# The operands of a pass made over two units, and two products changed about in the last unit

## The chip, the cores and the metric

The kernel runs on one core of a Trainium2 chip. Its engines work side by side, each on its own queue of instructions in a fixed order: TensorE (PE in the profile) multiplies, VectorE (DVE) and ScalarE (ACT) work element by element, GpSimd (POOL) and SyncE (SP) mostly issue DMAs here. An instruction waits until what it reads is there and until the buffer that it writes is free, and everything behind it on the same engine waits with it. The metric is the device time of one execution in microseconds (us); the times given are medians of several executions. One more execution was recorded by the profiler, and all rows in this document come from such recordings.

## The reference

Three networks stand behind one another. Cut to what matters, the computation is:

```python
x = attention(q, k, v)               # 4 x 8 heads x 576 x 64, local and strided masks
x = routed_experts(x, ...)           # 2304 tokens, 512 wide, 8 experts, one for each token
h = np.maximum(x @ w_in, 0.0)        # second network: 512 -> 2048
return (h * h @ w_out).astype(np.float32)   # 2048 -> 512
```

All the change lies in the last two lines: x has 2304 rows of 512, w_in is 512 x 2048, w_out is 2048 x 512.

## The kernel before

**Passes and units.** The second network runs in three passes, g = 0, 1, 2, of six tiles of 128 tokens each, in two halves of three tiles (384 tokens). A pass has eight units, c = 0 to 7; a unit computes 256 of the 2048 hidden columns and adds their part of the output. The trace names things of a unit by its number: m_7S is a product of unit 7, gl_7_10 an operand made from one of its results.

**Seven products.** A unit multiplies a 2 x 2 block matrix of weights (two blocks of 128 columns by two of 256 inputs) with a 2 x 2 block matrix of tokens, by a scheme of seven products of sums instead of eight: in this order A11·B11, S2·T2, A12·B21, S3·T3, S1·T1, A22·T4, S4·B22. In the trace m_7A is a product with a plain block A, m_7S one with a sum S. Each is six matmuls of 128 x 384 (function `mm3`, lines 1119 to 1121: every factor is a high part and a low part, and three of the four pairs are multiplied). The products lie in PSUM in two buffers, so that the sixth product may start only when what reads the fourth is done, and the seventh when what reads the fifth is done. VectorE joins the products with sums u (`add`, four tiles u[0] to u[3]): u[2] reads the fourth product, u[3] is the second reader of the fifth. In the trace all four are called u.

**Four results.** Four results, named by (i, hf) as 10, 01, 00, 11, go through `squared` (line 1432): VectorE adds a u into rl, ScalarE takes the relu and the square, gh is its high part (ScalarE), gl its low part (VectorE). Result 10 hangs on the third product, 01 on the fifth, 00 on the sixth, 11 on the seventh.

**The output.** `down` multiplies gh and gl with two rows of w_out (hwo, lwo: high and low part) into six PSUM tiles o_0 to o_5, one for each token tile, 36 matmuls of 128 x 512 in a unit; they accumulate over the eight units. These steps are spread through the next unit's products, as its `q()` calls come to them. With the last of them a tile is scaled into an SBUF buffer ob (even tiles on ScalarE, odd ones on VectorE), and POOL writes it to its rows of the output with an indirect DMA. There are five ob buffers, so a pass's sixth ob (ob_5) waits until the DMA of the first one has landed:

```python
ob = late.tile([P, D], F32, name=f"ob{g}_{t}", tag="ob", bufs=5)
```

**Operands of a pass.** The token sums of a pass are made by `split2(g, part)` from the transposed activations y2T: part 0 makes B11 and T2, part 1 B21 and T3, part 2 T1 and T4, part 3 B22. High parts (xh, xbh) are made by ScalarE, sums (xs) and low parts (xl, xbl) by VectorE; parts 0 to 2 take 2 xs or 4 xs of 384, one xl of 768 and two xl of 384, part 3 one xbl of 768. No DMA is in them. They are called in unit 7 of the pass before.

**Weights.** The weights of a unit come by DMA from a scratch in DRAM (SyncE's queue) and are split into high and low parts, hwa, hwb, hwo by ScalarE and lwa (128 x 1024), lwb (768), lwo (1024) by VectorE (line 1099).

**What sets the order.** The code is traced into a list, and a scheduler orders each engine's queue by its own estimates; `issue_after` and `keep_in_program_order` bind it in places. So a step that is called later may pull others with it.

Of the kernel before, what the change touches and what calls it, by code (L numbers as in the profile page):

```python
# [20 lines left out]
P = 128  # L21
# [6 lines left out]
F2 = 2048  # L28
# [5 lines left out]
UC = 256  # L34
# [21 lines left out]
MG = [(3, 3), (3, 3), (3, 3)]  # L56
# [75 lines left out]
def moe_kernel(ctx, tc, q, k, v, wg, wog, w1, w2, w_in64, w_out64, consts, out, dbg=None):  # L132
# [105 lines left out]
    lead = {}  # L238
# [630 lines left out]
    for b in range(B):  # L869
        t = tiles[b]  # L870
        tn = transposes(b + 1, tiles[b + 1]) if b + 1 < B else iter(())
        for n, ku in enumerate(ORDER[b].split()):
            kind, u = ku[0], int(ku[1:])
# [229 lines left out]
    def get(u):  # L1103
        assert u in ready
        return ready[u]

    def ahead(u, n, m=None, far=None):
        i = units.index(u)
        while nxt[0] < min(i + (far or n), len(units)):
            if nxt[0] >= i + n and units[nxt[0]][0] not in ("w1", "w2"):  # L1110
                break
            prep_unit(units[nxt[0]])
            nxt[0] += 1
        while cut[0] < min(i + (m or n), nxt[0]):
            split_unit(units[cut[0]])
            cut[0] += 1

    def mm3(ps, ah, al, bh, bl_, first, last, kept=lambda ins: ins):
        kept(nc.tensor.matmul(ps, ah, bh, start=first, stop=False))  # L1119
        kept(nc.tensor.matmul(ps, ah, bl_, start=False, stop=False))  # L1120
        lead["sum"] = kept(nc.tensor.matmul(ps, al, bh, start=False, stop=last))  # L1121
# [265 lines left out]
    for k in range(E):  # L1387
        for f in range(NF1):
# [22 lines left out]
            if (k, f) in CONV:  # L1411
                n = CONV.index((k, f))
# [5 lines left out]
            if f == (7 if k == 0 else 4) and k + 1 < E:  # L1418
                if k:
                    win_split(k + 1)  # L1420
                else:
                    a = pend.pop(0)
# [59 lines left out]
    def quarters(g, c, hs):  # L1482

        n = MG[g][0]
        if (g, c) == (len(MG) - 1, F2 // UC - 1):

            by = dict(hs)
            steps = [(i, 0, t) for i in (1, 0) for t in range(n)] + [(i, 1, t) for t in range(n, 2 * n) for i in (0, 1)]
            for i, hf, t in steps:
                yield lambda i=i, hf=hf, t=t: down(  # L1490
                    g, c * (UC // P) + i, [t], hf * n, by[i, hf], False, i == hf, tc.keep_in_program_order
                )
            return
        for (i, hf), h in hs:
            ts = range(hf * n, hf * n + n)
            first = c == 0 and (i, hf) in ((1, 0), (0, 1))
            last = c == F2 // UC - 1 and (i, hf) in ((0, 0), (1, 1))
            yield lambda i=i, ts=ts, h=h, a=first, b=last: down(g, c * (UC // P) + i, ts, ts[0], h, a, b)

    def m_unit(g, c, todo):  # L1500


        HC = MG[g][0] * P
        def preps(n):
            gate = lead.get("gate")
            with ExitStack() as st:
                for ins in gate or ():
                    st.enter_context(tc.issue_after(ins.ins))
                ahead(("wa", g, c), n)

        preps(3 if g + c == 0 else 5)
        wa, wb = get(("wa", g, c)), get(("wb", g, c))
        X = x2[g]
        q = lambda: next(todo, lambda: None)()
        end = c == F2 // UC - 1 and g + 1 < len(MG)

        def nxt_(part):
            if end:
                with tc.issue_after(lead["sq"][0].ins), tc.issue_after(lead["sq"][1].ins):
                    split2(g + 1, part)  # L1520

        def prod(w, x):
            j = BLK[w] - 1
            (wh, wl), j = (wa, j) if j < 4 else (wb, j - 4)
            xh, xl = X[x]
            ps = psm.tile([P, 512], F32, name=f"m{g}_{c}{w}", tag="h", bufs=2)
            for a in range(2):
                s_ = slice(a * P, (a + 1) * P)
                mm3(ps[:, :HC], wh[:, j, s_], wl[:, j, s_], xh[:, a], xl[:, a], a == 0, a == 1)
            return ps  # L1530

        u = [raws.tile([P, 3 * P], F32, name=f"u{i}{g}_{c}", tag="win", bufs=4)[:, :HC] for i in range(4)]
        add = lambda o, ps, x: nc.vector.tensor_tensor(o, ps[:, :HC], x, op=ALU.add)
        hs = []
        put = lambda i, hf, *a: hs.append(((i, hf), squared(f"{g}_{c}_{i}{hf}", *a)))
        p = prod("A11", "B11")
        nc.scalar.activation(u[0], p[:, :HC], AF.Copy)
        p = prod("S2", "T2")
        add(u[1], p, u[0])
        nxt_(0)  # L1540
        q()
        p = prod("A12", "B21")
        put(1, 0, p, HC, u[0])
        p = prod("S3", "T3")
        add(u[2], p, u[1])
        nxt_(1)
        q()
        p = prod("S1", "T1")
        put(0, 1, p, HC, u[2])
        if g == 0:  # L1550
            lead["gate"] = lead["sq"]
        else:
            lead.pop("gate", None)
        if g + c == 0:
            preps(5)
        add(u[3], p, u[1])
        p = prod("A22", "T4")
        put(0, 0, p, HC, u[2])
        nxt_(2)
        q()  # L1560
        p = prod("S4", "B22")
        put(1, 1, p, HC, u[3])
        nxt_(3)
        q()
        return quarters(g, c, hs)

    todo = iter([lambda a=a, d=d: e_l2(*a, range(d, d + 2)) for a in pend for d in (0, 2)])
    for g in range(len(MG)):
# [181 lines left out]
```

## Time and profile before

| what | value |
|---|---|
| median of 3 executions (lowest, highest) | 774.67 us (774.64, 775.0) |
| the profiled execution's own time | 773.4 us |
| its span, first to last instruction | 771.6 us |
| granted TensorE clock, mean | 0.998 of full speed |
| busy: PE, DVE, ACT, POOL | 98%, 72%, 60%, 22% of the span |

The span is what the rows count; 1.8 us of the execution lie outside it. PE is busy nearly all the time at nearly full clock, so the few places where it waits in the second network are what an order of work can change. Busy shares of the others are means over the whole run; near a change of pass they are much higher. The output's last DMA is issued by POOL at the end of the third pass.

### The profile page before, as it was taken

Reading aid. Unit: us, or ns where it says so; the run is one execution under the profiler, and the core shown is the slowest. Engines: PE = TensorE matmul, PEld = TensorE weight load, DVE = VectorE, ACT = ScalarE, POOL = GpSimd, SP = SyncE. Lnnn points to the kernel's source line nnn. Section 1 sums busy time; section 2 is a strip of 40 time slices with the busy share of each in tenths; the row PEclk is TensorE's granted clock in tenths of the full one; section 3 lists DMA queues with packets and bytes.
Section 4 is the critical chain, followed back from the end, with each engine's and each line's share of the span. In section 5 each row is a group of like instructions: output and inputs, shape, how many; then the busy total and the mean of one; then the engine's idle time right before and its main releaser. Section 6 shows DMA issues by size and latency. Waiting matters only on the chain.

```text
span 771.6 us, 14519 instructions
## 1 busy us (share of the span) xinstructions
PE 755.5 (98%) x5436; PEld 678.8 (88%) x5436; DVE 558.3 (72%) x1069; ACT 462.0 (60%) x935; POOL 171.5 (22%) x168
## 2 busy tenths in 40 slices
PE   8999999999999999999999999899999999999995
PEld 5777777999999999999988989788899888989894
DVE  4777787965676888898799888995455697555442
ACT  2764656425555555666687667785556676565443
POOL 6100002046528534320122222141000003000003
PEclk9999999999999999999999999999999999999999
DMA  9899715594988998965454544434222234222002
GB/s 207 170 199 228 143 58 152 185 299 146 202 265 192 329 282 277 305 205 183 157 205 151 177 148 171 157 136 157 91 76 96 86 118 159 78 93 103 1 0 84
DMA packets 104114, 124.86 MB, mean 162 GB/s; under 512 B 39428, under 2 KB 76856, under 8 KB 104040
## 3 DMA queue, kind: packets, MB, share of 16 engines
q1 hardware_dynamic: 95736, 100.42, 45.4%
q0 software_dynamic: 7568, 22.70, 8.9%
q8 instruction: 44, 0.72, 0.4%
q10 hardware_dynamic: 736, 0.76, 0.4%
q14 instruction: 30, 0.25, 0.1%
HBM read 101.82 MB, written 22.04 MB: 161 GB/s over the span
## 4 chain that ended last, share of the span: by engine, by line
PE 58%; issue 31%; DVE 6%; POOL 2%; DMA 1%; ACT 1%; SPq 0%; POOLq 0%; DVEq 0%; ACTq 0%
PE y L1119 5%; PE y L1121 5%; PE y L1120 5%; PE h L1119 5%; PE h L1121 5%; PE h L1120 5%; PE o L1120 2%; PE o L1119 2%; PE o L1121 2%; PE rw L566 2%; POOL out_dram L1471 2%; PE idle L232 1%; PE wt L1203 1%; PE lr L748 1%; PE sc2l L387 1%
## 5 line engine op out<-in xcount | busy, mean ns | idle before, releaser
L1119 PE MATMUL o<-hwo,gh 128*128 128x512 f32 x288 | 113.6, 396 | 0.4 <-ACT gh L1441 0.4
L1120 PE MATMUL o<-lwo,gh 128*128 128x512 f32 x288 | 113.5, 395 | 0.0
L1438 ACT ACTIVATE rl<-rl 128x384 f32<-128x384 f32 x96 | 49.6, 516 | 86.8 <-DVE rl L1436 86.8
L1099 DVE TENSOR_TENSOR lw<-rw,hw 128x1024 fp32r<-128x1024 f32 x62 | 83.0, 1341 | 16.3 <-ACT hw L1095 16.1
L1121 PE MATMUL o<-hwo,gl 128*128 128x512 f32 x288 | 84.2, 395 | 0.7 <-DVE gl L1443 0.7
L1119 PE MATMUL h<-xh,hw 128*128 128x416 f32 (+7 forms) x256 | 80.4, 315 | 0.2 <-DVE hl L1313 0.2
L1443 DVE TENSOR_TENSOR gl<-rl,gh 128x384 fp32r<-128x384 f32 x96 | 55.9, 585 | 32.6 <-ACT rl L1442 32.2
L1121 PE MATMUL h<-xh,lw 128*128 128x416 f32 (+7 forms) x256 | 79.3, 310 | 0.0
L1120 PE MATMUL h<-xl,hw 128*128 128x416 f32 (+7 forms) x256 | 79.3, 310 | 0.0
L1471 POOL DMA_INDIRECT out_dram<-ob,idx x18 | 23.1, 1284 | 252.3 <-ACT ob L1470 247.2
L1120 PE MATMUL y<-hl,hw 128*128 128x416 f32 (+7 forms) x256 | 78.6, 310 | 0.0
L1121 PE MATMUL y<-hh,lw 128*128 128x416 f32 (+7 forms) x256 | 78.1, 310 | 0.0
L1311 ACT ACTIVATE hh<-h 128x416 fp32r<-128x416 f32 (+7 forms) x64 | 28.2, 440 | 81.5 <-PE h L1121 81.5
L1119 PE MATMUL y<-hh,hw 128*128 128x416 f32 (+7 forms) x256 | 74.2, 311 | 0.0
L1095 ACT ACTIVATE hw<-rw 128x1024 fp32r<-128x1024 f32 x62 | 65.1, 1054 | 4.1 <-PE h L1120 3.8
L1119 PEld LDWEIGHTS o<-hwo,gh 128*128 128x128 f32 x288 | 54.0, 188 | 10.8 <-ACT gh L1441 1.2
L1120 PEld LDWEIGHTS o<-lwo,gh 128*128 128x128 f32 x288 | 54.1, 188 | 10.0 <-DVE lwo L1099 0.5
L1121 PEld LDWEIGHTS o<-hwo,gl 128*128 128x128 f32 x288 | 53.4, 188 | 8.7 <-DVE gl L1443 1.1
L1442 ACT ACTIVATE rl<-rl 128x384 f32<-128x384 f32 x96 | 50.1, 522 | 2.2
L1313 DVE SCALAR_TENSOR_TENSOR hl<-h,hh 128x416 fp32r<-128x416 f32 (+7 forms) x64 | 31.3, 489 | 27.5 <-ACT hh L1311 27.3
L1441 ACT ACTIVATE gh<-rl 128x384 fp32r<-128x384 f32 x96 | 50.0, 521 | 1.9
L1119 PEld LDWEIGHTS h<-xh,hw 128*128 128x128 f32 x256 | 48.2, 188 | 0.7 <-DVE hl L1313 0.5
(628 smaller groups left out, 1922.1 us busy)
## 6 DMA issues: line engine op xcount, KB each, us to landing
rw<-in_moe_w_dram SPq DMA_DIRECT2D x62, 512.0 KB, 5.7
rwa<-ws_d SPq DMA_DIRECT2D x24, 512.0 KB, 3.4
rwb<-ws_d SPq DMA_DIRECT2D x24, 384.0 KB, 3.2
e6wi<-in_moe_w_in_dram SPq DMA_DIRECT2D x32, 256.0 KB, 5.9
rwo<-wout_d SPq DMA_DIRECT2D x16, 512.0 KB, 3.6
x_d<-xr SPq DMA_DIRECT2D x18, 256.0 KB, 4.7
ws_d<-eo POOLq DMA_DIRECT2D x16, 256.0 KB, 5.2
s0wo<-in_moe_w_out_dram SPq DMA_DIRECT2D x8, 512.0 KB
```

Of the source, the lines that this page charges most:

```text
L1095: ia = nc.scalar.activation(hi, raw, AF.Copy)
L1099: iv = eng.tensor_tensor(lo, raw, hi.bitcast(F32), op=ALU.subtract)
L1119: kept(nc.tensor.matmul(ps, ah, bh, start=first, stop=False))
L1120: kept(nc.tensor.matmul(ps, ah, bl_, start=False, stop=False))
L1121: lead["sum"] = kept(nc.tensor.matmul(ps, al, bh, start=False, stop=last))
L1311: lead["relu"] = nc.scalar.activation(hh[:, :C], ps[:, :C], AF.Relu)
L1313: lead["step"] = nc.vector.scalar_tensor_tensor(out=hl[:, :C], in0=ps[:, :C], scalar=0.0, in1=hh[:, :C].bitcast(F32), op0=ALU.max, op1=ALU ...
L1438: nc.scalar.activation(rl[:, :HC], src, AF.Relu)
L1441: nc.scalar.activation(hh[:, :HC], rl[:, :HC], AF.Square)
L1442: ia = nc.scalar.activation(rl[:, :HC], rl[:, :HC], AF.Square)
L1443: iv = nc.vector.tensor_tensor(hl[:, :HC], rl[:, :HC], hh[:, :HC].bitcast(F32), op=ALU.subtract)
L1471: ins = nc.gpsimd.indirect_dma_start(out=out[:, :], out_offset=bass.IndirectOffsetOnAxis(ap=idx[:, gt_, 0:1], axis=0), in_=ob, in_offset=None,
```

## The change

Two things change. First, at the two changes of pass, only parts 0 and 1 of the next pass's operands are still called in unit 7 (at the first and the third of four places); parts 2 and 3 are called in the first unit of the new pass, at its first two places. Second, in the very last unit of the kernel the fifth and sixth products change places (A22·T4 comes before S1·T1), four steps of `down` are taken ahead of the seventh product, and the twelve last steps of `down` stand in another order.

```diff
--- before.py
+++ after.py
@@ -1484,11 +1484,12 @@
         n = MG[g][0]
         if (g, c) == (len(MG) - 1, F2 // UC - 1):
 
-            by = dict(hs)
-            steps = [(i, 0, t) for i in (1, 0) for t in range(n)] + [(i, 1, t) for t in range(n, 2 * n) for i in (0, 1)]
+            a, b, c_ = range(n, 2 * n)
+            steps = [(1, 0, t) for t in range(n)] + [(0, 0, t) for t in range(n)]
+            steps += [(0, 1, a), (0, 1, b), (1, 1, a), (1, 1, b), (0, 1, c_), (1, 1, c_)]
             for i, hf, t in steps:
                 yield lambda i=i, hf=hf, t=t: down(
-                    g, c * (UC // P) + i, [t], hf * n, by[i, hf], False, i == hf, tc.keep_in_program_order
+                    g, c * (UC // P) + i, [t], hf * n, dict(hs)[i, hf], False, i == hf, tc.keep_in_program_order
                 )
             return
         for (i, hf), h in hs:
@@ -1512,12 +1513,17 @@
         wa, wb = get(("wa", g, c)), get(("wb", g, c))
         X = x2[g]
         q = lambda: next(todo, lambda: None)()
-        end = c == F2 // UC - 1 and g + 1 < len(MG)
-
-        def nxt_(part):
-            if end:
+        very_last = (g, c) == (len(MG) - 1, F2 // UC - 1)
+
+        def nxt_(at):
+            to = g, None
+            if c == F2 // UC - 1 and g + 1 < len(MG):
+                to = g + 1, {0: 0, 2: 1}.get(at)
+            elif c == 0 and g:
+                to = g, {0: 2, 1: 3}.get(at)
+            if to[1] is not None:
                 with tc.issue_after(lead["sq"][0].ins), tc.issue_after(lead["sq"][1].ins):
-                    split2(g + 1, part)
+                    split2(*to)
 
         def prod(w, x):
             j = BLK[w] - 1
@@ -1545,24 +1551,32 @@
         add(u[2], p, u[1])
         nxt_(1)
         q()
-        p = prod("S1", "T1")
-        put(0, 1, p, HC, u[2])
-        if g == 0:
-            lead["gate"] = lead["sq"]
-        else:
-            lead.pop("gate", None)
-        if g + c == 0:
-            preps(5)
-        add(u[3], p, u[1])
-        p = prod("A22", "T4")
-        put(0, 0, p, HC, u[2])
-        nxt_(2)
-        q()
+        for part in ((0, 0), (0, 1)) if very_last else ((0, 1), (0, 0)):
+            if part == (0, 0):
+                p = prod("A22", "T4")
+                put(0, 0, p, HC, u[2])
+                nxt_(2)
+                q()
+                continue
+            p = prod("S1", "T1")
+            put(0, 1, p, HC, u[2])
+            if g == 0:
+                lead["gate"] = lead["sq"]
+            else:
+                lead.pop("gate", None)
+            if g + c == 0:
+                preps(5)
+            add(u[3], p, u[1])
+        rest = quarters(g, c, hs)
+        if very_last:
+            q()
+            for _ in range(MG[g][0] + 1):
+                next(rest)()
         p = prod("S4", "B22")
         put(1, 1, p, HC, u[3])
         nxt_(3)
         q()
-        return quarters(g, c, hs)
+        return rest
 
     todo = iter([lambda a=a, d=d: e_l2(*a, range(d, d + 2)) for a in pend for d in (0, 2)])
     for g in range(len(MG)):
```

**First place: VectorE, end of unit 7 of the first pass.** Rows before, from the gl of result 10 on (u_7_… are sums u, xl_1 and xs_1 belong to part 1 of the next pass, rl_7_01, rl_7_00 and rl_7_11 to this unit's results, lw… to weights):

```order
L1443 TENSOR_TENSOR gl_7_10_6735<-rl_7_10_6731,gh_7_10_6734 128x384
L1343 TENSOR_TENSOR xl_1_6748<-y2T,xh_1_6747 128x768
L1353 TENSOR_TENSOR xs_1_0_6751<-y2T 128x384
L1353 TENSOR_TENSOR xs_1_1_6755<-y2T 128x384
L1436 TENSOR_TENSOR rl_7_01_6775<-m_7S_6768,u_7_6683 128x384
L1533 TENSOR_TENSOR u_7_6684<-m_7S_6768,u_7_6682 128x384
L1436 TENSOR_TENSOR rl_7_00_6791<-m_7A_6784,u_7_6683 128x384
L1343 TENSOR_TENSOR xl_1_6748<-xs_1_0_6751,xh_1_6747 128x384
L1343 TENSOR_TENSOR xl_1_6748<-xs_1_1_6755,xh_1_6747 128x384
L1436 TENSOR_TENSOR rl_7_11_6829<-m_7S_6822,u_7_6684 128x384
L1443 TENSOR_TENSOR gl_7_01_6779<-rl_7_01_6775,gh_7_01_6778 128x384
```

The same place after:

```order
L1443 TENSOR_TENSOR gl_7_10_6735<-rl_7_10_6731,gh_7_10_6734 128x384
L1436 TENSOR_TENSOR rl_7_01_6763<-m_7S_6756,u_7_6683 128x384
L1539 TENSOR_TENSOR u_7_6684<-m_7S_6756,u_7_6682 128x384
L1436 TENSOR_TENSOR rl_7_00_6779<-m_7A_6772,u_7_6683 128x384
L1436 TENSOR_TENSOR rl_7_11_6815<-m_7S_6808,u_7_6684 128x384
L1443 TENSOR_TENSOR gl_7_01_6767<-rl_7_01_6763,gh_7_01_6766 128x384
```

The five instructions of part 1 (two xs, three xl) have left this place; the second sum u of it (u[3]) stands two rows behind gl instead of five.

**Second place: VectorE, unit 0 of the second pass.** Before, from xbl (part 3) to the last ob of the first pass; the second sum u_0 here, behind rl_0_01, is u[3]:

```order
L1343 TENSOR_TENSOR xbl_6838<-y2T,xbh_6837 128x768
L1533 TENSOR_TENSOR u_0_6870<-m_0S_6912,u_0_6869 128x384
L1468 TENSOR_SCALAR ob_1_6969<-o_1_5718,idx 128x512
L1343 TENSOR_TENSOR xl_2_6800<-xs_2_0_6803,xh_2_6799 128x384
L1343 TENSOR_TENSOR xl_2_6800<-xs_2_1_6808,xh_2_6799 128x384
L1468 TENSOR_SCALAR ob_3_6996<-o_3_5720,idx 128x512
L1436 TENSOR_TENSOR rl_0_01_6936<-m_0S_6929,u_0_6870 128x384
L1533 TENSOR_TENSOR u_0_6871<-m_0S_6929,u_0_6869 128x384
L1468 TENSOR_SCALAR ob_5_7008<-o_5_5722,idx 128x512
```

After, from the last xl of part 1 to u[3], which now stands behind ob_5, lwo_1 and xs of part 2; ahead of these rows, since rl_7_11, also stand the rest of part 1 and the first xl of part 2:

```order
L1343 TENSOR_TENSOR xl_1_6788<-xs_1_1_6795,xh_1_6787 128x384
L1353 TENSOR_TENSOR xs_2_0_6874<-y2T 128x384
L1468 TENSOR_SCALAR ob_5_7008<-o_5_5722,idx 128x512
L1099 TENSOR_TENSOR lwo_1_7019<-rwo_1_7011,hwo_1_7017 128x1024
L1353 TENSOR_TENSOR xs_2_1_6879<-y2T 128x384
L1353 TENSOR_TENSOR xs_2_0_6874<-xs_2_0_6874,xt_6703 128x384
L1539 TENSOR_TENSOR u_0_6852<-m_0S_6908,u_0_6851 128x384
L1443 TENSOR_TENSOR gl_0_10_6904<-rl_0_10_6900,gh_0_10_6903 128x384
L1343 TENSOR_TENSOR xbl_6917<-y2T,xbh_6916 128x768
L1353 TENSOR_TENSOR xs_2_1_6879<-xs_2_1_6879,xt_6703 128x384
L1436 TENSOR_TENSOR rl_0_01_6936<-m_0S_6929,u_0_6852 128x384
L1539 TENSOR_TENSOR u_0_6853<-m_0S_6929,u_0_6851 128x384
```

Counted from rl_7_11, u[3] of this unit was the 22nd instruction and is the 28th. TensorE, the same unit, around the seventh product (the one that reads xbh), before:

```order
L1120 MATMUL m_0A_6945<-xl_2_6800,hwa_0_6673 128x384
L1121 MATMUL m_0A_6945<-xh_2_6799,lwa_0_6675 128x384
L1119 MATMUL m_0A_6945<-xh_2_6799,hwa_0_6673 128x384
L1120 MATMUL m_0A_6945<-xl_2_6800,hwa_0_6673 128x384
L1121 MATMUL m_0A_6945<-xh_2_6799,lwa_0_6675 128x384
L1119 MATMUL m_0S_6978<-xbh_6837,hwb_0_6677 128x384
L1120 MATMUL m_0S_6978<-xbl_6838,hwb_0_6677 128x384
L1121 MATMUL m_0S_6978<-xbh_6837,lwb_0_6679 128x384
L1119 MATMUL m_0S_6978<-xbh_6837,hwb_0_6677 128x384
```

and after, where the sixth product (m_0A with xh_2, xl_2) is cut in pieces that stand on both sides of the seventh:

```order
L1119 MATMUL m_0A_6945<-xh_2_6870,hwa_0_6673 128x384
L1121 MATMUL o_0_7049<-hwo_0_6838,gl_0_10_6904 128x512
L1121 MATMUL o_1_7050<-hwo_0_6838,gl_0_10_6904 128x512
L1121 MATMUL o_2_7051<-hwo_0_6838,gl_0_10_6904 128x512
L1119 MATMUL m_0S_6978<-xbh_6916,hwb_0_6677 128x384
L1120 MATMUL m_0S_6978<-xbl_6917,hwb_0_6677 128x384
L1121 MATMUL m_0S_6978<-xbh_6916,lwb_0_6679 128x384
L1119 MATMUL m_0S_6978<-xbh_6916,hwb_0_6677 128x384
L1120 MATMUL m_0S_6978<-xbl_6917,hwb_0_6677 128x384
L1121 MATMUL m_0S_6978<-xbh_6916,lwb_0_6679 128x384
L1120 MATMUL m_0A_6945<-xl_2_6871,hwa_0_6673 128x384
```

After them TensorE has the rest of m_0A and the nine matmuls of gh and gl of result 01, then the first product of unit 1; the three of gl of result 01 came behind that product before.

**Third place: ScalarE, change from the second pass to the third.** The ob_0 and ob_2 of the second pass up to the high half of lwo's partner (hwo_1), before:

```order
L1470 ACTIVATE ob_0_8175<-o_0_7049,idx 128x512
L1470 ACTIVATE ob_2_8187<-o_2_7051,idx 128x512
L1342 ACTIVATE xh_2_8011<-xs_2_0_8015 128x384
L1342 ACTIVATE xh_2_8011<-xs_2_1_8020 128x384
L1438 ACTIVATE rl_0_10_8116<-rl_0_10_8116 128x384
L1441 ACTIVATE gh_0_10_8119<-rl_0_10_8116 128x384
L1442 ACTIVATE rl_0_10_8116<-rl_0_10_8116 128x384
L1470 ACTIVATE ob_4_8214<-o_4_7053,idx 128x512
L1095 ACTIVATE hwo_1_8229<-rwo_1_8223 128x1024
```

After:

```order
L1470 ACTIVATE ob_0_8175<-o_0_7049,idx 128x512
L1470 ACTIVATE ob_2_8187<-o_2_7051,idx 128x512
L1470 ACTIVATE ob_4_8214<-o_4_7053,idx 128x512
L1095 ACTIVATE hwo_1_8229<-rwo_1_8223 128x1024
L1342 ACTIVATE xh_2_8082<-xs_2_0_8086 128x384
L1438 ACTIVATE rl_0_10_8112<-rl_0_10_8112 128x384
L1441 ACTIVATE gh_0_10_8115<-rl_0_10_8112 128x384
```

ob_4 and hwo_1 (with its 1024 columns) have come ahead of the relu and the square of result 10 of the third pass's first unit, and one xh has gone behind them. SyncE's queue is the same before and after. On POOL, at the first change of pass only, ob_1's DMA has come ahead of ob_0's.

## Rows read from the trace of the kernel before

**Rows 1.** Windows: stretch, length, each engine's busy us (instructions), PE clock, DMA share, GB/s

```profile
485.00:523.00 38.00, 35.82 (x173) 30.80 (x172) 37.34 (x58) 30.25 (x54) 13.27 (x9) 1.00 0.47 161
...
628.00:646.00 18.00, 17.79 (x87) 15.36 (x86) 18.00 (x31) 15.18 (x28) 6.22 (x6) 1.00 0.36 126
```

**Rows 2.** Waits of PE, 455 to 772: waited for, total us, times, longest

```profile
PE m_7S L1119 <- DVE u L1533: 1.2, 1, 1.2
PE o L1121 <- DVE gl L1443: 0.7, 1, 0.7
...
PE o L1119 <- ACT gh L1441: 0.4, 2, 0.2
```

**Rows 3.** Timeline of PE: start, us, instruction, [idle before <-releaser]

```profile
499.44 0.86 PE L1121 MATMUL o<-hwo,gl 128*128 128x512 f32 x3
501.48 0.44 PE L1119 MATMUL m_7S<-xbh,hwb 128*128 128x384 f32 x1 [1.18 <-DVE u L1533]
501.76 0.34 PE L1120 MATMUL m_7S<-xbl,hwb 128*128 128x384 f32 x1
...
516.61 0.33 PE L1119 MATMUL m_0S<-xbh,hwb 128*128 128x384 f32 x1
...
520.22 0.34 PE L1119 MATMUL m_1A<-xh,hwa 128*128 128x384 f32 x1
```

**Rows 4.** Timeline of DVE, first pass change

```profile
498.60 0.96 DVE L1343 TENSOR_TENSOR xl<-y2T,xh 128x768 fp32r<-128x768 f32 x1
...
500.40 0.56 DVE L1436 TENSOR_TENSOR rl<-m_7S,u 128x384 f32<-128x384 f32 x1
500.87 0.56 DVE L1533 TENSOR_TENSOR u<-m_7S,u 128x384 f32<-128x384 f32 x1
...
502.83 0.56 DVE L1436 TENSOR_TENSOR rl<-m_7S,u 128x384 f32<-128x384 f32 x1
...
503.89 1.23 DVE L1099 TENSOR_TENSOR lwo<-rwo,hwo 128x1024 fp32r<-128x1024 f32 x1
...
514.58 0.75 DVE L1468 TENSOR_SCALAR ob<-o,idx 128x512 f32<-128x512 f32 x1
...
515.70 0.55 DVE L1533 TENSOR_TENSOR u<-m_0S,u 128x384 f32<-128x384 f32 x1
```

**Rows 5.** Timeline of POOL, output DMAs

```profile
637.64 2.00 POOL L1471 DMA_INDIRECT out_dram<-ob,idx  x1 [114.41 <-ACT ob L1470]
...
758.74 0.97 POOL L1471 DMA_INDIRECT out_dram<-ob,idx  x1 [111.59 <-ACT ob L1470]
...
765.12 0.97 POOL L1471 DMA_INDIRECT out_dram<-ob,idx  x1 [0.30 <-ACTq L1722]
```

**Rows 6.** Chain of waits, 630 to 660: start, us, what

```profile
637.64 3.76 DMA out_dram<-ob,idx
```

**Rows 7.** Output DMAs as a group: issue to landing

```profile
DMA to landing us min/median/max: 2.7/3.6/5.9
```

**Rows 8.** Timeline of PE, second pass change

```profile
645.16 0.34 PE L1121 MATMUL m_0S<-xbh,lwb 128*128 128x384 f32 x1
645.69 0.50 PE L1119 MATMUL o<-hwo,gh 128*128 128x512 f32 x1 [0.19 <-ACT gh L1441]
```

**Rows 9.** Timeline of ACT, second pass change

```profile
639.21 0.53 ACT L1441 ACTIVATE gh<-rl 128x384 fp32r<-128x384 f32 x1
...
641.09 0.69 ACT L1470 ACTIVATE ob<-o,idx 128x512 f32<-128x512 f32 x1 [0.80 <-PE o L1121]
641.68 1.05 ACT L1095 ACTIVATE hwo<-rwo 128x1024 fp32r<-128x1024 f32 x1
```

**Rows 10.** Timeline of PE, last unit

```profile
754.91 0.34 PE L1119 MATMUL m_7S<-xbh,hwb 128*128 128x384 f32 x1
...
755.96 0.39 PE L1119 MATMUL o<-hwo,gh 128*128 128x512 f32 x1
...
757.24 0.50 PE L1121 MATMUL o<-hwo,gl 128*128 128x512 f32 x1 [0.65 <-DVE gl L1443]
```

## The prediction

> **What bounds the kernel now.** I read the busy shares first: TensorE is busy 98% of the span at nearly full clock, so time can only come from the places where it waits. The view of TensorE's waits over the second network [rows 2] names few: 1.2 us ahead of a seventh product for a sum u on VectorE, 0.7 ahead of an output matmul for a gl, and 0.4 in two waits for a gh. The timeline places the first [rows 3]: the seventh product of unit 7 of the first pass starts at 501.48. Three matmuls of 512 columns start at 499.44 and take 0.86 together; one alone takes 0.39 [rows 10], so they follow each other at 0.235 (0.233 over longer runs of them), and TensorE would have been there at 500.14. So the lag is 1.34. What follows a wait is slow too: 501.48 to 501.76 is 0.28, where a 384-column step is 0.175 (755.96 less 754.91, over six [rows 10]). In all I count 4.3 us of such lags in the second network; no gain can be larger.
>
> Next, the windows [rows 1]: around both changes of pass VectorE is busy 37.34 of 38 us and 18.00 of 18. There VectorE's queue, not TensorE's, sets when things are ready, and I read order there as time: what stands ahead of a sum u delays it by its slot. Slots are durations less the overlap of 0.09 that 500.40 and 500.87 show (0.56 long, 0.47 apart) [rows 4]: 0.47 for 384 columns, 0.87 for 768, 1.14 for 1024 (the 1.23 of lwo), 0.66 for an ob.
>
> **The change, first change of pass.** In unit 7 the rows of part 1 leave the place behind the gl. That gl ends its slot at 498.60, where an xl of part 1 stood. Now rl is at 498.60, u[3] at 499.07, done by 499.62, ahead of TensorE's 500.14. The 1.34 goes away. The seventh product then frees rl_7_11 at 502.83 − 1.34 − 0.10 = 501.39 (0.10 is the slow step). Part 1 isn't gone, though: it is 2 × 0.47 + 0.87 + 2 × 0.47 = 2.75 us of VectorE's work that now stands behind this point.
>
> From rl_7_11 to u[3] of the next unit VectorE had 21 rows that lasted from 502.83 to 515.70, 12.87 us [rows 4]. After, 27 rows stand there, by the order: 17 of 384 columns (7.99), three of 1024 (3.42), four of 768 (3.48), three ob (1.98), 16.87 in sum. Beside part 1 they hold ob_5, lwo_1 and a gl that stood behind u[3] before (0.66 + 1.14 + 0.47); two xl of part 2 went behind it (0.94). So u[3] starts at 501.39 + 16.87 = 518.26. To this comes what ob_5 waits for its buffer: ob_1's DMA is now the first. By the slots ob_1 is done near 508.96, POOL issues 0.27 later, and the landing of a pass's first output took 3.76 at the other change [rows 6]; that is 512.99, and ob_5's slot begins at 512.75, so some 0.2. u[3] ends near 519.0, and the seventh product of unit 0 starts there.
>
> TensorE, unhindered from 500.14, needs for 37 matmuls of 384 and 36 of 512 up to that product 6.48 + 8.39 = 14.87, and would be there at 515.0. Now it waits 3.9, in part already at the sixth product, which needs u[2]. In before it came through this place with a seventh product at 516.61 without a wait. From the seventh product to the first matmul of unit 1 TensorE has 11 of 384 and 9 of 512, 4.02: 523.0. Before that was 520.22, with three matmuls of 512 fewer done (0.70). The balance is 523.0 − 520.22 − 0.70 = **+2.1**. Behind this point TensorE's waits name nothing until the second change [rows 2], so I take nothing more as handed on.
>
> **Second change of pass.** Two queues are longer. On ScalarE ob_4 and hwo_1 now stand ahead of the relu and square of result 10. From the start of o_4's last matmul: 0.48 until ob_4 starts, then slots of 0.59 and 0.95 (0.69 and 1.05 less the 0.10 of 641.09 to 641.68 [rows 9]), 0.43 for an xh, 0.55 for the relu and 0.53 for gh: 3.53. TensorE has by the order two matmuls of 512 and twelve of 384 up to the one that reads gh, 2.57. It waits 0.96. On VectorE u[3] stands behind ob_5, which waits for ob_0's landing. From the start of o_0's last matmul: eviction 1.11, POOL 0.27, landing 3.76 [rows 6] make 5.14; behind ob_5 come 0.66, 0.47, 0.47, 1.14, 0.47, 0.47, and u[3] itself 0.55: 9.37. TensorE reaches the seventh product 3.38 + 3.53 + 2.2 = 9.11 behind the same point: 0.3 late. An xl behind u[3] makes the rest of the sixth product 0.25 late. In all 1.5. Before, the lags here were 0.35 (the row at 645.16 leads to 645.34, the next came at 645.69 [rows 8]) and two small ones of 0.07 and 0.18. The balance is **+0.9**.
>
> The 3.76 is one landing; the group of 18 has 2.7, 3.6 and 5.9 as lowest, median and highest [rows 7]. At 2.7 ob_5 doesn't wait, and this place costs 0.96 − 0.60 = +0.4, the first +1.9. At 5.9 ob_5 holds VectorE some 2.2 us longer, at either place.
>
> How long POOL works on an issue bears on that: 2.00 us at 637.64, with VectorE full, and 0.97 at 758.74, with it idle for much of the time [rows 1, 5]. The Trainium skill, SBUF — State Buffer, "Who interferes with whom", says that a VectorE instruction with two inputs in SBUF contends with a GpSimd instruction that reads SBUF, and its section "SBUF: two separate sides" warns that descriptors for GpSimd's DMAs can be held up by VectorE. By that rule denser VectorE work beside the first issue would make the landing later, which is rival A; the two issue rows agree with its sign, and don't show the cause.
>
> **The last unit.** With A22·T4 first, gl of result 00 is ready early, and the wait of 0.65 at 757.24 goes [rows 10]. By the order o_0's last matmul is now fifth behind the seventh product: 755.96 + 4 × 0.233 = 756.89, and the eviction may start 0.40 later, at 757.29; before, at 757.24 + 0.50 = 757.74. POOL's six issues run from 758.74 to 765.12 one behind the other [rows 5] and stay the end: o_5's last matmul leaves about 1 us to the last issue. So **−0.45**; the other 0.3 to 0.4 that TensorE saves is cover.
>
> **Sum.** 2.1 + 0.9 − 0.45 = +2.6. All slots are from the profiled execution, 773.4 (1.8 outside the span of 771.6), which would become 776.0; the median of 774.67 lies 1.27 higher, as executions vary, so I add the difference to it: **777.3**. Matmuls, elementwise work and DMAs are the same in number and size, so no other price changes. SyncE's queue is the same.
>
> **The rivals.**
> A. Later landing. If the first output of a pass lands after 5.9 instead of 3.76 us, ob_5 stands at the head of VectorE's queue 2.1 us longer and u[3], lwo_1 and all behind it with it: +2.1 at one change or both, 779.4 to 781.5. For it: the denser VectorE. Against: the first landings are the only ones that count, and the one in the chain was 3.76.
> B. Part of the losses fails to come: landing at 2.7, and ScalarE catches up because its slots ahead of ob_4 are empty. Then the second change gives its old lags back, −0.6 instead of +0.9, and the first costs +1.9: 1.9 − 0.6 − 0.45 = +0.85, 775.5, within measurement. Against: the wait for gh is a sum of fixed slots.
> C. Faster. The split takes part 1 from unit 7 and unit 0 absorbs it. All that is named goes: 1.34 and the 0.37 of the first gh, 0.60, and 0.45 at the end: −2.8, 771.9. It decides at one point: u[3] of unit 0 must end by 515.0, not 519.0. Before, it ended at 516.25 with 21 rows ahead; it would need 4 us of holes in VectorE's stretch, and [rows 1] leave 0.66 in 38.
> That the change does not do what it says is out: the order shows the rows moved.
>
> **How the numbers follow.** A difference under 0.2%, 1.55 us, is about what a measurement of this kernel can't tell from none. I give the forecast 0.62 (776.2 to 778.8), A 0.17, B 0.13, C 0.08. Forecast and A lie above 776.22, less 0.02 for the forecast's low edge; B and that edge within; C below. So slower 0.77, same 0.15, faster 0.08. The range goes down to 775.0, which takes in B, and up to 779.8, which takes in A at one change; A at both and C are left out.
>
> **What would show it.** In the profile after: no wait of the seventh product in unit 7 of the first pass, its start near 500.1; VectorE without a hole up to u[3] of the next unit, which starts near 518.4; TensorE's waits for u there near 3.5 us in sum, the largest new ones; a wait for gh near 0.9 at the second change, and ob_5 there just behind ob_0's landing; no wait for gl in the last unit, the six issues still 6.4 us apart from first to last. The prediction is wrong if u[3] comes before 515.5 (C), or if ob_5 waits more than 1.5 us (A).

## The result, and the profile after

| kernel | median, us | executions | granted clock of the executions | ratio to before (95% interval) |
|---|---|---|---|---|
| before, beside it | 775.0 (774.07 to 778.37) | 9 | | |
| changed | 781.2 (779.19 to 783.6) | 9 | 0.989 to 0.995 | 1.0079 (1.0066 to 1.0093) |

The change makes the kernel slower by 6.2 us. The forecast was 777.3 with a range up to 779.8: the sign was right, the size not. The profiled execution took 779.19, its span is 777.3 (771.6 before).

The waits of TensorE in the second network, in total, times and longest:

```profile
PE m_0A L1119 <- ACT xh L1342: 1.8, 1, 1.8
PE m_0S L1119 <- DVE rl L1436: 1.3, 1, 1.3
PE o L1119 <- ACT gh L1441: 1.2, 2, 0.8
PE m_7A L1119 <- DVE u L1539: 0.6, 1, 0.6
```

Both waits that [rows 2] named first are gone: u in unit 7 and gl in the last unit. New are 1.8 and 1.3 us in unit 0, and a wait of 0.8 for a gh at the second change. In the timeline of TensorE the first change reads so:

```profile
500.54 0.34 PE L1119 MATMUL m_7S<-xbh,hwb 128*128 128x384 f32 x1
...
513.87 0.50 PE L1119 MATMUL o<-hwo,gh 128*128 128x512 f32 x1 [0.47 <-ACT gh L1441]
...
517.34 0.43 PE L1119 MATMUL m_0A<-xh,hwa 128*128 128x384 f32 x1 [1.81 <-ACT xh L1342]
...
519.99 0.69 PE L1119 MATMUL m_0S<-xbh,hwb 128*128 128x384 f32 x1 [1.29 <-DVE rl L1436]
520.47 0.52 PE L1120 MATMUL m_0S<-xbl,hwb 128*128 128x384 f32 x1
...
525.75 0.45 PE L1119 MATMUL m_1A<-xh,hwa 128*128 128x384 f32 x1
```

The seventh product of unit 7 starts at 500.54, without a wait; everything in this execution is 0.40 later than in [rows 3] before the change begins (the sixth product of unit 7 started at 498.67 instead of 498.27), so this is the 500.14 of the forecast. The seventh product of unit 0 starts at 519.99, which is 519.59 in the forecast's time; 519.0 was forecast. From there to the first matmul of unit 1, at 525.75, it takes 5.76 us. For the same 20 matmuls the forecast had 4.02. The step from 519.99 to 520.47 is 0.48 where it was 0.28 behind a wait in [rows 3]. VectorE at the same place:

```profile
499.48 0.54 DVE L1539 TENSOR_TENSOR u<-m_7S,u 128x384 f32<-128x384 f32 x1
...
501.78 0.56 DVE L1436 TENSOR_TENSOR rl<-m_7S,u 128x384 f32<-128x384 f32 x1 [1.18 <-PE m_7S L1121]
...
513.91 0.75 DVE L1468 TENSOR_SCALAR ob<-o,idx 128x512 f32<-128x512 f32 x1 [0.71 <-DMA out_dram<-ob,idx]
...
519.38 0.55 DVE L1539 TENSOR_TENSOR u<-m_0S,u 128x384 f32<-128x384 f32 x1
```

u[3] of unit 7 is at 499.48 and of unit 0 at 519.38. Between them ob_5 waited 0.71 for the landing of ob_1. The waits' view puts the second wait down to a rl; it is u[3], the next row, whose end at 519.93 releases the product. The first and longer wait, 1.81, is the sixth product's. The forecast named u[2] for it, which ends at 517.19. What ended last is xh of part 2, at 517.28; ScalarE made it from an xs that VectorE had ready only at 516.73. Both hang on the same full queue of VectorE:

```profile
516.18 0.55 DVE L1353 TENSOR_TENSOR xs<-xs,xt 128x384 f32<-128x384 f32 x1
516.64 0.55 DVE L1539 TENSOR_TENSOR u<-m_0S,u 128x384 f32<-128x384 f32 x1
```

```profile
516.76 0.52 ACT L1342 ACTIVATE xh<-xs 128x384 fp32r<-128x384 f32 x1 [1.65 <-DVE xs L1353]
```

The windows (length, busy time of TensorE, weight loads, VectorE, ScalarE, GpSimd with instructions, then the granted clock, DMA share, GB/s) say why the 20 matmuls took so long:

```profile
512.00:520.00 8.00, 4.43 (x19) 2.76 (x18) 7.29 (x14) 4.54 (x8) 5.85 (x6) 1.00 0.61 217
520.00:526.00 6.00, 6.00 (x21) 5.29 (x22) 3.52 (x6) 3.17 (x6) 0.00 (x0) 0.72 0.18 64
520.00:522.00 2.00, 2.00 (x6) 2.00 (x7) 1.42 (x3) 1.08 (x4) 0.00 (x0) 0.50 0.30 115
```

Up to 520 TensorE was busy 4.43 of 8 us; in the next 6 us its granted clock averages 0.72, with 0.50 from 520 to 522: the lower one of its two levels, 1.2 instead of 2.4 GHz. Before, the clock was 1.00 throughout this place [rows 1].

The second change of pass, TensorE:

```profile
645.28 0.34 PE L1121 MATMUL m_0S<-xh,lwa 128*128 128x384 f32 x1
646.40 0.50 PE L1119 MATMUL o<-hwo,gh 128*128 128x512 f32 x1 [0.78 <-ACT gh L1441]
...
648.41 0.34 PE L1119 MATMUL m_0A<-xh,hwa 128*128 128x384 f32 x1
648.59 0.35 PE L1119 MATMUL m_0S<-xbh,hwb 128*128 128x384 f32 x1
648.90 0.44 PE L1120 MATMUL m_0A<-xl,hwa 128*128 128x384 f32 x1
```

It arrives at 645.28 + 0.175 and goes on at 646.40, 0.95 late, for a gh. The seventh product at 648.59 is on time; the rest of the sixth comes 0.14 late, at 648.90. VectorE's ob_3 and ob_5 there, and then GpSimd's first issue of each pass, and the second and the last issue of the last pass:

```profile
643.36 1.56 DVE L1468 TENSOR_SCALAR ob<-o,idx 128x512 f32<-128x512 f32 x2
```

```profile
509.63 2.43 POOL L1471 DMA_INDIRECT out_dram<-ob,idx  x1 [18.60 <-DVE ob L1468]
...
640.89 1.32 POOL L1471 DMA_INDIRECT out_dram<-ob,idx  x1 [121.52 <-ACT ob L1470]
...
763.62 0.97 POOL L1471 DMA_INDIRECT out_dram<-ob,idx  x1 [113.92 <-ACT ob L1470]
764.89 1.29 POOL L1471 DMA_INDIRECT out_dram<-ob,idx  x1 [0.30 <-issue]
...
770.31 0.97 POOL L1471 DMA_INDIRECT out_dram<-ob,idx  x1 [0.30 <-issue]
```

Two ob in 1.56 us instead of 1.42: ob_5 hardly waited for the landing of what was issued at 640.89. At the end the first issue comes 3.40 us behind the last seventh product (760.22), before 3.83 [rows 5, 10]; the second took 1.29 instead of 0.97, so that the last issue gains only 0.1.

### The profile page after: what moved, and what is told of

The parts are those of the page before. It is cut to its first block, busy times and chain, and to the rows that moved or that the text cites. A ratio compares the mean times of both kernels' runs of the same rounds, so it can differ in the third digit from the quotient of the medians.

```text
span 777.3 us, 14524 instructions
## 1 busy us (share of the span) xinstructions
PE 757.1 (97%) x5436; PEld 680.0 (87%) x5436; DVE 559.2 (72%) x1069; ACT 461.9 (59%) x935; POOL 170.6 (22%) x168
## 4 chain that ended last, share of the span: by engine, by line
PE 88%; DVE 3%; issue 3%; DMA 3%; ACT 1%; POOL 1%; SPq 0%; ACTq 0%; POOLq 0%; DVEq 0%
PE o L1119 8%; PE o L1120 8%; PE o L1121 8%; PE y L1119 5%; PE y L1120 5%; PE y L1121 5%; PE h L1119 5%; PE h L1121 5%; PE h L1120 5%; PE rw L566 2%; PE wt L1203 1%; PE lr L748 1%; DMA msk<-in_consts_dram 1%; PE sc2l L387 1%; PE m_1S L1120 1%
## 5 line engine op out<-in xcount | busy, mean ns | idle before, releaser
L1471 POOL DMA_INDIRECT out_dram<-ob,idx x18 | 21.4, 1187 | 258.9 <-ACT ob L1470 235.4
L1120 PEld LDWEIGHTS y<-hl,hw 128*128 128x128 f32 x256 | 48.2, 188 | 1.0 <-issue 0.9
```

Source lines behind the costliest of these rows:

```text
L1471: ins = nc.gpsimd.indirect_dma_start(out=out[:, :], out_offset=bass.IndirectOffsetOnAxis(ap=idx[:, gt_, 0:1], axis=0), in_=ob, in_offset=None,
```

## The experiments

**Which part costs.** Three kernels have one part each, one has the split without the last unit's change, and the changed kernel ran once more beside them. The last unit alone (e_last) has the parts as before:

```diff
+        end = c == F2 // UC - 1 and g + 1 < len(MG)
+
         def nxt_(at):
-            to = g, None
-            if c == F2 // UC - 1 and g + 1 < len(MG):
-                to = g + 1, {0: 0, 2: 1}.get(at)
-            elif c == 0 and g:
-                to = g, {0: 2, 1: 3}.get(at)
-            if to[1] is not None:
+            if end:
                 with tc.issue_after(lead["sq"][0].ins), tc.issue_after(lead["sq"][1].ins):
-                    split2(*to)
+                    split2(g + 1, at)
```

> The last unit's change alone, all four parts of the operands in unit 7 as in the kernel before. If the loss comes from the changes of pass: -0.45 us against the kernel before (about 774.5 where it is 775.0), no wait for gl in the last unit, TensorE's waits at both changes of pass as before (1.34 us of lag in unit 7, no clock below 1.00 there). If a part of the loss is the last unit's: above 776.

The split alone (e_split) has the products and the steps of the last unit of the kernel before (the steps are not shown again); e_split1 and e_split2 limit it further to one change of pass (G is 1 or 2):

```diff
-        very_last = (g, c) == (len(MG) - 1, F2 // UC - 1)
+        very_last = False
...
-                to = g + 1, {0: 0, 2: 1}.get(at)
-            elif c == 0 and g:
+                to = g + 1, {0: 0, 2: 1}.get(at) if g + 1 == G else at
+            elif c == 0 and g == G:
```

> The split over two units at the first change of pass alone, the second change and the last unit as before. Theory (VectorE's queue makes TensorE wait some 3.6 us in unit 0, and TensorE's clock then falls to half for some 3 us): +4.4 us or more against before, 779.5 to 781, with a stretch of granted clock near 0.5 right behind the seventh product of unit 0. Rival (the loss is spread over both changes in equal parts and the clock is an accident of one execution): about +3, 778, clock 0.998.

> The split at the second change of pass alone. Theory (no wait there is long, TensorE's clock stays): +0.3 to +0.9 us against before, waits of TensorE for gh near 0.9 to 1.2 us at the second change, granted clock 1.00 there. Rival (each change of pass costs the same): +2.8.

> The split over two units at both changes of pass, the last unit as before. If parts add up: the changed kernel less 0 to 0.5 us. Rival (the last unit's new order is what makes the difference between +3 and +6): 2 us or more faster than the changed kernel.

> The changed kernel once more, beside the others and on their chip; the line of what single parts cost there (+2.8 for the first change of pass, +0.5 for the last unit, and the second change to come) makes +4 if parts add up; +6 if the first comparison's size belongs to the kernel and the parts don't add up. In the profile: the seventh product of unit 0 of the second pass 19.0 to 19.6 us behind that of unit 7, and a stretch of half clock behind it.

| kernel | median, us | before beside it | ratio (95% interval) | granted clock |
|---|---|---|---|---|
| e_last | 773.88 | 773.37 | 1.0008 (0.9999 to 1.0017) | 0.996 to 0.998 |
| e_split1 | 776.2 | 773.37 | 1.0032 (1.0020 to 1.0044) | 0.992 to 0.997 |
| e_split2 | 775.25 | 773.48 | 1.0022 (1.0010 to 1.0034) | 0.996 to 0.998 |
| e_split | 779.17 | 773.48 | 1.0074 (1.0056 to 1.0091) | 0.993 to 0.995 |
| changed, again | 778.79 | 773.48 | 1.0070 (1.0053 to 1.0087) | 0.991 to 0.997 |

The last unit's change is not told from nothing: 0.5 us slower alone, 0.4 faster on top of the split. In the profile of e_last the wait for gl is gone, and the last issue comes 10.06 us behind the last seventh product instead of 10.21; what lies behind the last issue is 7.28 long instead of 6.48, and in four executions of the changed kernel it is 6.23 to 6.99. A gain of 0.15 can't be seen behind that.

The split is the whole loss. Its two places cost 2.8 and 1.8 us alone, and both forecasts were missed. The three parts alone make 5.1 in sum, the changed kernel beside them 5.3, so they about add up; the +4 of the last forecast counted the second change too low. For e_split1 the theory had said +4.4 or more. Its profile shows what the theory said of the first change: the same two waits (1.80 and 1.31), a clock of 0.72 from 520 to 526, and 5.78 us from the seventh product of unit 0 to unit 1. But the end of that execution is only 2.7 behind that of before. A part alone is scheduled anew, and its later places are not those of the changed kernel: the wait for gl in the last unit, 0.65 before, is gone there too, and what lies behind the last issue took 5.70.

e_split2 was to cost 0.3 to 0.9. Its profiled execution is 0.9 us of span over that of before, at a clock of 1.00 throughout the second change; no profile shows what the rest of the 1.8 of the median is. The gh at the second change is awaited 1.1 us instead of 0.8 (the 1.3 hold 0.2 of the first change):

```profile
PE o L1119 <- ACT gh L1441: 1.3, 2, 1.1
```

**With and without a fall of the clock.** The profiled execution of the changed kernel in its second comparison took 776.51 at a clock of 0.997. Its timeline of TensorE:

```profile
500.15 0.34 PE L1119 MATMUL m_7S<-xbh,hwb 128*128 128x384 f32 x1
...
516.98 0.44 PE L1119 MATMUL m_0A<-xh,hwa 128*128 128x384 f32 x1 [1.81 <-ACT xh L1342]
...
519.63 0.44 PE L1119 MATMUL m_0S<-xbh,hwb 128*128 128x384 f32 x1 [1.30 <-DVE u L1539]
...
523.86 0.45 PE L1119 MATMUL m_1A<-xh,hwa 128*128 128x384 f32 x1
```

and its windows:

```profile
512.00:520.00 8.00, 4.42 (x18) 2.74 (x18) 7.29 (x14) 4.51 (x9) 5.79 (x5) 1.00 0.67 228
520.00:526.00 6.00, 6.00 (x32) 5.29 (x31) 4.18 (x7) 4.74 (x9) 0.00 (x0) 1.00 0.33 103
```

The waits are the same 1.81 and 1.30, TensorE is busy 4.42 of 8 us, and the seventh product of unit 0 follows that of unit 7 after 19.48 us (19.45 in the first profile). But the clock stays at 1.00, and the 20 matmuls take 523.86 − 519.63 = 4.23. Two more profiled executions of the same kernel:

> The changed kernel, one profiled execution: either without a fall of the clock (776.5, seventh product of unit 0 followed by unit 1 after 4.2 us) or with one (778 to 779, 5.8 us); if it is above 780, the records show where else the clock falls.

> As the look before it, one more execution of the changed kernel.

They took 780.03 and 778.61, both at a mean clock of 0.991. The windows of the first:

```profile
512.00:520.00 8.00, 4.41 (x19) 2.74 (x17) 7.28 (x14) 4.50 (x9) 5.80 (x5) 0.94 0.61 217
520.00:526.00 6.00, 6.00 (x17) 5.43 (x18) 2.58 (x4) 2.09 (x3) 0.00 (x0) 0.51 0.18 48
```

Here the clock is 0.51 over the 6 us. The four profiled executions in order (starts of the seventh products of units 7 and 0 and of unit 1, in us):

| execution | clock | unit 7 | unit 0 | unit 1 | unit 0 to 1 | its time |
|---|---|---|---|---|---|---|
| first | 0.995 | 500.54 | 519.99 | 525.75 | 5.76 | 779.19 |
| second | 0.997 | 500.15 | 519.63 | 523.86 | 4.23 | 776.51 |
| third | 0.991 | 500.43 | 519.91 | 526.86 | 6.95 | 780.03 |
| fourth | 0.991 | 499.63 | 519.08 | 525.64 | 6.56 | 778.61 |

The way to the seventh product is the same within 0.03 us; what lies behind it differs by up to 2.7, with the clock. In windows of 13 us over each of these four executions, the clock is 1.00 everywhere else but behind TensorE's last matmul, where a fall costs nothing. That last stretch is in the mean clock too, so the mean alone doesn't tell a fall in unit 0: 0.995 stands beside one in the first execution, and beside none in the profile of the next experiment.

Two of the kernels above have the same waits in unit 0. In the profile of e_split the same 20 matmuls took 5.79 us, in that of e_split1 5.78. So the clock fell behind these waits in five of six profiles. In the profiles of before, e_last and e_split2, which don't have them, it held.

**Filling the wait.** Twelve more matmuls stand ahead of where TensorE would wait; `prod` is given an instruction after which its matmuls are issued. Cut to what matters:

```diff
+        def junk(n):
+            ins, wh = lead["sum"], get(("wo", g, c))[0]
+            for _ in range(n):
+                with tc.issue_after(ins.ins):
+                    ins = nc.tensor.matmul(obk[g][4], X["B11"][0][:, 0, :P], wh[:, 0, :], start=True, stop=True)
+            lead["junk"] = ins
...
-        def prod(w, x):
+        def prod(w, x, after=None):
...
-                p = prod("A22", "T4")
+                if (g, c) == (1, 0):
+                    junk(FILL[0])
+                p = prod("A22", "T4", lead.pop("junk", None))
...
-        p = prod("S4", "B22")
+        if (g, c) == (1, 0):
+            junk(FILL[1])
+        p = prod("S4", "B22", lead.pop("junk", None))
```

FILL is 7, 5.

> The changed kernel with twelve more matmuls of 128x512 on TensorE in unit 0 of the second pass, ahead of the rest of the fourth product, where TensorE would wait later. They write to the PSUM tile o_4 before its first real product overwrites it, so the output is the same; 2.8 us of work more. Theory (the clock falls because TensorE waits): the waits in unit 0 shrink from 3.6 to under 1.2 us, the clock stays at 1.00 there, and the kernel is 1.5 us or more faster than the changed one although it does more: 778 to 779.5. Rival (VectorE's queue and the late landing are all, the clock does not hang on the waits): within 0.5 us of the changed kernel, 781, or slower, with the same stretch at 0.5.

Measured: 777.15 (before 773.37; 1.0041, 1.0028 to 1.0054), clocks 0.995 to 0.997 in five executions, 776.27 to 778.12. In the profile all twelve stand in one group from 513.30 to 516.10. Its windows, and the seventh product of unit 7 and the start of unit 1:

```profile
512.00:520.00 8.00, 7.11 (x34) 5.61 (x32) 7.29 (x14) 4.55 (x8) 6.29 (x6) 1.00 0.59 199
520.00:526.00 6.00, 5.86 (x29) 5.15 (x30) 5.14 (x9) 5.39 (x10) 0.00 (x0) 1.00 0.20 67
```

```profile
500.97 0.34 PE L1119 MATMUL m_7S<-xbh,hwb 128*128 128x384 f32 x1
...
524.50 0.34 PE L1119 MATMUL m_1A<-xh,hwa 128*128 128x384 f32 x1
```

TensorE is busy 7.11 of the 8 us, the clock stays at 1.00, unit 1 starts 23.5 us behind the seventh product of unit 7 (500.97 to 524.50), and by the ratios (1.0041 and 1.0070) the kernel is 2.2 us faster than the changed one although it does 2.8 us of work more. What is left of the waits in unit 0 is one of 0.9. The way to unit 1 is that of the execution without a fall (23.7), so nearly all of the gain is the clock's. One profile alone could be the one in six without a fall; the ratio over five executions and the next experiment say the same, though. With the waits filled or shortened the clock held, so the fall hangs on them. Whether on their sum, on the longest or on their nearness, these runs don't separate.

**VectorE's order.** ob_5 of the first two passes is put behind u[3]:

```diff
-                    nc.vector.tensor_scalar(ob, obk[g][t], sc, None, op0=ALU.mult)
+                    with tc.issue_after(lead["u3"].ins) if t == 5 else nullcontext():
+                        nc.vector.tensor_scalar(ob, obk[g][t], sc, None, op0=ALU.mult)
...
-            add(u[3], p, u[1])
+            lead["u3"] = add(u[3], p, u[1])
```

> The changed kernel with ob_5 of the first two passes put behind u[3] on VectorE; nothing else at the first change moves ahead of u[3]. Theory (u[3] is as late as the slots ahead of it): u[3] 1.37 us earlier (the 0.66 of ob_5 and the 0.71 that it waited for a landing), TensorE's waits in unit 0 from 3.6 to 2.2; 1.4 us faster than the changed kernel if the clock still falls (779.8), up to 3 us if it doesn't (778). Rival (only the landing counts): 0.7 us. Rival (another queue ends last there, so that u[3] doesn't matter): no change, 781.

Measured: 776.77 (1.0038, 1.0025 to 1.0051), clocks 0.995 to 0.997; by the ratios 2.5 us faster than the changed kernel. VectorE's u[3] and ob_5, and TensorE's seventh products of units 7 and 0 and its unit 1:

```profile
518.66 0.55 DVE L1540 TENSOR_TENSOR u<-m_0S,u 128x384 f32<-128x384 f32 x1
...
519.59 0.74 DVE L1469 TENSOR_SCALAR ob<-o,idx 128x512 f32<-128x512 f32 x1
```

```profile
501.24 0.34 PE L1119 MATMUL m_7S<-xbh,hwb 128*128 128x384 f32 x1
...
519.26 0.44 PE L1119 MATMUL m_0S<-xbh,hwb 128*128 128x384 f32 x1 [1.30 <-DVE u L1540]
...
523.50 0.44 PE L1119 MATMUL m_1A<-xh,hwa 128*128 128x384 f32 x1
```

u[3] starts at 518.66, 17.4 us behind the seventh product of unit 7 (501.24), in the changed kernel 18.84: 1.42 earlier for a forecast of 1.37. The seventh product of unit 0 follows at 519.26, and unit 1 starts at 523.50, so that the clock held in this execution (1.00 in all windows there). The waits in unit 0 are 0.47, 0.34 and 1.30, 2.1 in sum for a forecast of 2.2. Both rivals fall: the time moved, and u[3] came earlier by twice what the landing alone would give.

**A smaller split.** Only part 3 goes to the new pass, with the last unit's change kept:

```diff
-                to = g + 1, {0: 0, 2: 1}.get(at)
+                to = g + 1, {0: 0, 1: 1, 2: 2}.get(at)
             elif c == 0 and g:
-                to = g, {0: 2, 1: 3}.get(at)
+                to = g, {1: 3}.get(at)
```

> Parts 0 to 2 in unit 7 as before, only part 3 (xbl, xbh of B22) called in the first unit of the new pass, at its second place; the last unit as changed. By the order u[3] of unit 0 then has fewer VectorE rows ahead of it than in the kernel before (xbl and one ob stand behind it), and the gh that TensorE waited for at both changes comes earlier. Theory (order around u[3] and gh sets the time): the lags of 0.37 and 0.35 at the two changes go, the 1.34 in unit 7 stays: 0.7 us faster than before, more or less 0.5 for the last unit. Rival (any part called in the new pass costs): slower than before by 1 us or more.

> The variant with only part 3 in the new pass and the changed last unit, once more: 0.4 us faster than before if the first comparison holds; its interval there still took in no change.

Measured: 773.1 beside 773.48 (0.9991, 0.9979 to 1.0002), then 773.11 beside 773.57 (1.0005, 0.9994 to 1.0017). TensorE's waits:

```profile
PE m_7S L1119 <- DVE u L1539: 1.2, 1, 1.2
PE m_7A L1119 <- DVE u L1539: 0.6, 1, 0.6
PE m_7S L1119 <- DVE rl L1436: 0.2, 1, 0.2
```

The two waits for gh are gone, as expected. The rival's loss of 1 us or more did not come; but the time doesn't tell the kernel from the one before, and a gain of 0.4 to 0.7 us lies below what these comparisons tell. To take the 1.2 in unit 7 as well, two sums of part 1 were given to GpSimd:

```diff
-                sub(t, x[:, a], y[:, a])
+                eng = nc.gpsimd if (g, part) == (1, 1) else nc.vector
+                eng.tensor_tensor(t, x[:, a], y[:, a], op=ALU.subtract)
```

> The same, and at the first change of pass the two first sums of part 1 (xs of 128x384) are made by GpSimd instead of VectorE, which takes 0.94 us off VectorE ahead of u[3] in unit 7. Theory (VectorE's slots ahead of u[3] set the 1.34 of lag there): the seventh product's lag in unit 7 falls to some 0.4, 0.9 us faster than the variant without it. Rival (GpSimd is slow or holds VectorE up, so that xl of these sums and with them u[3] or the third product come later): no gain or a loss, with VectorE's instructions beside them longer than 0.56.

Measured: 774.16 beside 773.57 (1.0010, 0.9998 to 1.0021). VectorE, GpSimd's two sums, and the wait of the seventh product:

```profile
497.83 0.89 DVE L1444 TENSOR_TENSOR gl<-rl,gh 128x384 fp32r<-128x384 f32 x1
498.64 1.77 DVE L1343 TENSOR_TENSOR xl<-y2T,xh 128x768 fp32r<-128x768 f32 x1
...
500.81 0.54 DVE L1540 TENSOR_TENSOR u<-m_7S,u 128x384 f32<-128x384 f32 x1
```

```profile
497.13 2.47 POOL L1368 TENSOR_TENSOR xs<-y2T 128x384 f32<-128x384 f32 x2 [6.82 <-DVE xl L1343]
```

```profile
PE m_7S L1119 <- DVE u L1540: 1.4, 1, 1.4
```

While GpSimd works on its sums, from 497.13 to 499.60, VectorE's gl takes 0.89 instead of 0.55 and its xl of 768 columns 1.77 instead of 0.96. That is 1.15 us, more than the 0.94 taken away. u[3] starts 2.98 behind that gl, where it was 2.74 in the variant without it (497.73 to 500.47), and the wait of the seventh product is 1.4 instead of 1.2. The rival held in these rows; in the medians the loss is not told from nothing. The Trainium skill, SBUF — State Buffer, "Who interferes with whom", has this rule: a VectorE instruction with two inputs in SBUF contends with a GpSimd instruction that reads SBUF. These rows agree.

## Why the prediction was wrong

**The step that failed** is the sentence that no other price changes, and with it the 4.02 us from the seventh product of unit 0 to unit 1. The sum counted a wait at its length. In three of four profiled executions of the changed kernel the granted clock fell to its lower level around or behind the waits in unit 0, and the same 20 matmuls took 5.76, 6.95 and 6.56 us. That is 1.5 to 2.7 us over the 4.23 of the execution without a fall. Filling the waits took the fall away, which shows that it hangs on them. Why the same waits bring it in one execution and not in another, no run here shows. The forecast put this term at nothing without a reason, and no rival had it. All that its rows showed of it was a clock of 1.00 beside a single wait of 1.2 us [rows 1, 2]. The Trainium skill, TensorE: Matmul & The Clock Gate, "HAM oscillation — how this bites in real kernels", tells of a kernel in which waits for DMAs of some 3 to 5 us each put TensorE back to its lower clock, so that the work behind them starts slow. The traces agree in three of four on what follows a wait, and differ on its length: the longest here was 1.81.

**The first change of pass** was right in mechanism and order. The 1.34 in unit 7 went away, and u[3] of unit 0 came late for the rows ahead of it. The view's waits there are 3.6 us in sum, near the 3.5 that were named as the sign, though only 1.3 of them are for a u. Counted as the forecast counted its 3.9 (519.0 − 515.0 makes 4.0), the seventh product is 19.45 − 14.87 = 4.6 late. Without a fall of the clock unit 1 starts 23.71 us behind the seventh product of unit 7. Before, counted from 500.14, where that product would have stood without its lag, it was 520.22 − 500.14 + 0.70 = 20.78. The balance is +2.9 for a forecast of +2.1. Of the difference 0.5 is ob_5's wait, 0.71 for 0.2 (ob_5 starts 4.28 us behind the issue at 509.63; the forecast had a landing of 3.76), and 0.2 are longer steps behind the seventh product (4.23 for 4.02). With a fall the balance is 4.4 to 5.7.

**The second change** came out at +0.3 for +0.9 (unit 1 of the second pass to unit 1 of the third, 126.60 in the execution without a fall; before 126.97 − 0.70). The wait for gh was 0.95 for 0.96. The 0.3 of the seventh product did not come, since ob_5 hardly waited for ob_0's landing. The lags of before held some 0.3 of longer steps more than I counted, those of after 0.2.

**The last unit**: 0.43 for 0.45 at the first issue, then lost at the second. The medians show nothing of it.

**The sum** of the execution without a fall is 774.7 − 771.6 = +3.1 us of span, for a forecast of +2.6. That it comes so near is in part luck: the first change cost 0.8 more, the second 0.6 less. A fall of the clock adds 1.5 to 2.7, which makes 4.6 to 5.8. The second comparison's +5.3 lies in that, the first one's +6.2 a little above it. The span also holds what lies behind the last issue, which differs by up to 0.8 between the four executions, so a single one doesn't settle the rest. Of the nine executions of the first comparison those with a mean clock of 0.995 lie at 779.19 to 780.36, the one with 0.989 at 783.6; all executions of before that ran beside the experiments have 0.995 to 0.998. Two profiles with a mean of 0.991 show the fall in unit 0 and no other ahead of TensorE's last matmul. The execution at 783.6 has no profile.

**The rivals.** C needed u[3] to end by 515.0, and it ended at 519.5 in the forecast's time. For B the landing at the second change was early enough, but the wait for gh came in full and the 1.9 of the first change was exceeded. The measured 781.2 lies among A's times, but not by A's mechanism: it would have needed landings of 5.9 and a wait of ob_5 of more than 1.5. ob_5 waited 0.71, and it came 4.28 us behind the issue at the first change and 3.3 at the second. A full VectorE by itself doesn't lengthen an issue either: at the first change, with VectorE busy beside both, GpSimd's first issue took 2.43 and its fifth 0.97.

## What to carry to other kernels

Where a queue is full, work that is taken from one place lands ahead of something else: count the slots up to the instruction that the busiest engine waits for, in the new order. Price a new wait of TensorE at its length and, as a second case, with the matmuls behind it at half clock; here it came with waits of 0.47, 1.81 and 1.30 us within 6.6 us, and not with a single one of 1.2. A range should hold both.

## What the runs showed of the hardware

The same program with the same waits (1.81 the longest) kept its clock in one execution and lost it in three, for 3.4 to 6.8 us at 0.50 (the share below 1.00 of the windows, over 0.5). Of all 14 profiles, five of the six with these waits show a fall ahead of TensorE's last matmul, and none of the other eight. One issue of an indirect DMA on GpSimd took from 0.97 to 2.43 us in the changed kernel. From the last issue to the end of the span it took 6.23 to 6.99 us in four executions of one program. Two subtractions of 128 x 384 on GpSimd (2.47 us) made VectorE's beside them 1.6 to 1.8 times as long.
